# Rearranging the prologue of a sketched attention with feed-forward, and eight products on a tile of ones for TensorE

**The chip, the cores and the metric.** The kernel runs on one core of a Trainium2 chip. The metric is the device time of one execution in microseconds (us). A profile's span is about 1.8 us shorter than the time of the same execution (327.3 beside 329.06 us in the kernel before).

## The reference

The program is a sketched attention (batch 4, 4 heads, 1088 rows, 32 columns per head), whose output is the input of a gated feed-forward block on 4352 tokens.

```python
# S1, S2: 8 x 32 sketches; phi(x) = outer(S1 x, S2 x), 64 features
q_p, k_p = (phi(q), phi(k))
kv = np.einsum('bhsf,bhsd->bhfd', k_p, v)
z = np.sum(k_p, axis=2)
num = np.einsum('bhsf,bhfd->bhsd', q_p, kv)
den = np.einsum('bhsf,bhf->bhs', q_p, z)[..., None] + 1e-06
x = (num / den)                      # then to (4352, 128)
gate = 1.0 / (1.0 + np.exp(-(x @ w_gate)))
out = (gate * (x @ w_val)) @ w_out   # 128 -> 1536 -> 128
```

S1, S2 and the three weights come as 64-bit floats, which the kernel makes narrow with integer operations; the rest is 32-bit.

## The kernel before

The attention of one batch gives the tokens that the feed-forward block takes in chunks of 512. A chunk takes twelve waves: in a wave TensorE makes gate and value of one block of 128 hidden columns, ScalarE the sigmoid (`sg`), VectorE the product (`g`), and later TensorE adds it into `moeout`. The attention of later batches is done between waves. Before the first wave of all stands a prologue with nothing of the feed-forward block to fill it. Its order, the same for every engine, is that of the program:

```python
    # S is loaded (both on SyncE), made narrow, transposed, masked to sk ...
    turn_k(0, ((0, KBASE[2] + 1), (KBASE[2] + 1, T)))   # VectorE: kT, two parts
    turn_q(0, 0)                                        # VectorE: qT
    kps(0)                  # TensorE: kps = sk.T kT;  VectorE: kab = its transpose
    ab((0, 0, 0))           # TensorE: aps;  ScalarE: asb = copy of aps
    mult00 = ab((0, 1, 0), (0, 0, 0))
    mult10 = ab(None, (0, 1, 0), (psm, "wave"))
    for j0, j1 in ((0, 5), (5, NJK)):
        outer(0, 3, j0, j1)                             # GpSimd: kp of the last head
        for h in range(3):
            outer(0, h, j0, j1, nc.vector)              # VectorE: kp of three heads
        if j0 == 0:
            kv(0, [1, 2, 3, 4])                         # TensorE: kvz += v.T kp
    mult00()                                            # VectorE: qp = aps * bps
    mult10()
    kv(0, [5, 6, 7, 8, 0])                              # ... then ScalarE: kvd
    narrow_w(0, 0)
    narrow_w(1, 0)
    narrow_w(0, 1)
    ndt(0)                  # TensorE: ndps = kvd.T; VectorE: zb; ScalarE: nd
    narrow_w(2, 0)
    narrow_w(3, 0)
    invert = den(0, 0)      # TensorE: dps = zb.T qp
    divide = num(0, 0)      # TensorE: nps = nd.T qp
    invert()                # VectorE: dT, rc, rb
    divide()                # VectorE: xT = nps * rb
    narrow_w(0, 2)          # VectorE: w_sb of block 0
    narrow_w(1, 1)
    turn_q(0, 1)

    slot(None, 1)           # the first wave
    slot(lambda: r_group((0, 0, 1), None), 1)
    # ... cut ...
```

The narrowing of a tile is a chain over three engines, cut in steps by `yield`:

```python
        # step 0: cap (VectorE or GpSimd), tail (ScalarE)
        # step 1: two VectorE instructions make head, then:
        nc.scalar.activation(out=cap.bitcast(F32), in_=cap.bitcast(F32), func=ACTF.Square)
        nc.gpsimd.tensor_tensor(out=head, in0=head, in1=tail, op=ALU.add)
        yield
        # step 2: VectorE writes the narrow tile
```

The products of a wave and of `aps` and one of the `bps` share two buffers of PSUM (pool `psm`, tag `wave`), so one begins when the one before the last has been read.

Of the kernel before, what the change touches and what calls it, by code (L numbers as in the profile page):

```python
# [8 lines left out]
F32 = mybir.dt.float32  # L9
# [3 lines left out]
ALU = mybir.AluOpType  # L13
ACTF = mybir.ActivationFunctionType
MUL = ALU.mult

P = 128
# [3 lines left out]
def kernel(  # L21
# [12 lines left out]
    nc = tc.nc  # L34
# [11 lines left out]
    NJK = 9  # L46
# [34 lines left out]
    def narrow(out, bits, eng):  # L81




        n, m = out.shape[1:]
        lo, hi = bits[:, :, :, 0].bitcast(U32), bits[:, :, :, 1]

        def tmp(dt, tag, bufs):
            return sbN.tile([P, 3, P], dt, tag=tag, name=tag, bufs=bufs)[:, :n, :m]  # L90



        cap, tail = tmp(I32, "cap", 5), tmp(I32, "tail", 4)
        eng.tensor_scalar(
            out=cap.bitcast(F32), in0=hi.bitcast(F32), scalar1=122880.0, scalar2=-122880.0,
            op0=ALU.min, op1=ALU.max,
        )
        nc.scalar.activation(out=tail, in_=lo, func=ACTF.Copy, scale=2.0**-29)
        yield  # L100

        head = tmp(I32, "head", 3)
        nc.vector.tensor_scalar(  # L103
            out=head, in0=cap, scalar1=3, scalar2=0x3FFFFFF8,
            op0=ALU.logical_shift_left, op1=ALU.bitwise_and,
        )
        nc.vector.scalar_tensor_tensor(  # L107
            out=head, in0=cap, scalar=-0x40000000, in1=head, op0=ALU.bitwise_and, op1=ALU.bitwise_or
        )
        nc.scalar.activation(out=cap.bitcast(F32), in_=cap.bitcast(F32), func=ACTF.Square)  # L110
        nc.gpsimd.tensor_tensor(out=head, in0=head, in1=tail, op=ALU.add)  # L111
        yield

        nc.vector.scalar_tensor_tensor(  # L114
            out=out, in0=cap.bitcast(F32), scalar=1.265625 * 2.0**-30, in1=head.bitcast(F32),
            op0=ALU.is_ge, op1=MUL,
        )
        yield
# [3 lines left out]
    for n, s_ in enumerate((S1, S2)):  # L122
        rows = bass.AP(tensor=s_.tensor, offset=s_.offset, ap=[[0, P // R], [D, R], [1, D]])
        if wide:
            nc.sync.dma_start(
                out=sr_in[:, n].rearrange("p d w -> p (d w)"), in_=rows.bitcast(I32)
            )
        else:
            nc.sync.dma_start(out=sr[:, n], in_=rows)


    w_sb = const.tile([P, 3, NJ, P], F32, tag="w_sb", name="w_sb")
# [82 lines left out]
    ones = const.tile([P, 32], F32, tag="ones")  # L215
    nc.vector.memset(ones, 1.0)

    sig0 = const.tile([P, 1], F32, tag="sig0")
    nc.scalar.activation(out=sig0, in_=ones[:, :1], func=ACTF.Sigmoid)
    hm = const.tile([P, 2, R], F32, tag="hm")  # L220
    nc.vector.memset(hm, 0.0)
    for h in range(H):
# [4 lines left out]
    for n in range(2):  # L227
        t = const.tile([P, H, 32], F32, tag=f"zb{n}", name=f"zb{n}")
        nc.gpsimd.memset(t, 0.0)
        zb.append(t)  # L230

    if wide:
        for _ in narrow(sr, sr_in, nc.vector):
            pass

    sk = const.tile([P, 2, 2, R], F32, tag="sk")
    sab = []
    for n, inner in enumerate(([[1, R], [0, R]], [[0, R], [1, R]])):
        st_ = const.tile([P, 4, R], F32, tag=f"st{n}", name=f"st{n}")
        nc.vector.transpose(out=st_.rearrange("p u r -> p (u r)"), in_=sr[:, n])  # L240
        nc.vector.tensor_tensor(out=sk[:, :, n, :], in0=st_[:, :2, :], in1=hm, op=MUL)
        t = const.tile([P, R, R], F32, tag=f"s{n}", name=f"s{n}")
        nc.scalar.copy(
            out=t, in_=bass.AP(tensor=st_.tensor, offset=st_.offset, ap=[list(st_.ap[0])] + inner)
        )
        sab.append(t.rearrange("p i j -> p (i j)"))
    sa, sb = sab
    sk = sk.rearrange("p m n r -> p (m n r)")

    xT = const.tile([P, NTOK], F32, tag="xT")  # L250

# [37 lines left out]
    def w1():  # L289

        ci = moe["ci"]
        t0, tw = tok_chk[ci]
        jn = TCH // tw
        j0 = moe["w"] * jn
        wv = psm.tile([P, 2, TCH], F32, tag="wave", name="wave")
        if ci == 0:
            narrow_w(j0 + 4, 0)
            narrow_w(j0 + 2, 1)
            narrow_w(j0 + 1, 2)
        for which in range(2):  # L300
            for jj in range(jn):
                nc.tensor.matmul(  # L302
                    out=wv[:, which, jj * tw : (jj + 1) * tw],
                    lhsT=w_sb[:, which, j0 + jj, :],
                    rhs=xT[:, t0 : t0 + tw],
                    start=True,
                    stop=True,
                )
        sg = sbG.tile([P, TCH], F32, tag="sg", name="sg", bufs=3)
        nc.scalar.activation(out=sg, in_=wv[:, 0], func=ACTF.Sigmoid)  # L310


        def glu():
            g = sbG.tile([P, TCH], F32, tag="g", name="g")
            nc.vector.tensor_tensor(out=g, in0=wv[:, 1], in1=sg, op=MUL)  # L315
            moe["todo"].append((ci, j0, jn, g.rearrange("p (j t) -> p j t", j=jn)))

        moe["gate"] = glu
        moe["w"] += 1
        if j0 + jn == NJ:  # L320
            moe["ci"] += 1
            moe["w"] = 0
# [27 lines left out]

    kT_of, qT_of = {}, {}

    def turn_k(b, parts=((0, T),)):
        if b >= B:
            return
        kT = sbA.tile([P, T, 32], F32, tag="kT", name="kT")
        for t0, t1 in parts:
            nc.vector.transpose(  # L358
                out=kT[:, t0:t1].rearrange("p t s -> p (t s)"),
                in_=k_t[b][:, t0:t1].rearrange("p t d -> p (t d)"),  # L360
            )
        kT_of[b] = kT.rearrange("p t s -> p (t s)")

    def turn_q(b, n):
        if b >= B:
# [11 lines left out]
    def kps(b):  # L377
        t = ps2.tile([P, 2, 512], F32, tag="two", name="kps")
        for g in range(4):
            for pi in range(2):  # L380
                rows = slice(64 * pi, 64 * pi + 64)
                nc.tensor.matmul(  # L382
                    out=t[32 * g : 32 * g + 32, pi, : NJK * 32],
                    lhsT=sk[rows, :],
                    rhs=kT_of[b][rows, KBASE[g] * 32 : (KBASE[g] + NJK) * 32],
                    start=True,
                    stop=True,
                )

        KAB[b] = sbA.tile([P, 2, NJK, 32], F32, tag="kab", name="kab")  # L390
        for pi in range(2):
            nc.vector.transpose(  # L392
                out=KAB[b][:, pi].rearrange("p j c -> p (j c)"), in_=t[:, pi, : NJK * 32]
            )
        KP[b] = sbA.tile([P, H, NJK, F], F32, tag="kp", name="kp")

    def outer(b, h, j0=0, j1=NJK, eng=nc.gpsimd):
        a0 = KAB[b][:, h // 2, j0:j1, 2 * R * (h % 2) :]
        pst = list(a0.ap[0])
        jn = j1 - j0  # L400
        eng.tensor_tensor(  # L401
            out=KP[b][:, h, j0:j1].rearrange("p j (i l) -> p j i l", i=R),
            in0=bass.AP(tensor=a0.tensor, offset=a0.offset, ap=[pst, [32, jn], [1, R], [0, R]]),
            in1=bass.AP(tensor=a0.tensor, offset=a0.offset + R, ap=[pst, [32, jn], [0, R], [1, R]]),
            op=MUL,
        )

# [44 lines left out]
    def kv(b, j_list, zsum=None):  # L452
# [4 lines left out]
        for j in j_list:  # L457
            kr = 64 if j == 0 else P
            for which in range(2 if zsum is None else 1):
                for h in range(H):  # L460
                    nc.tensor.matmul(  # L461
                        out=kvz[32 * h : 32 * h + 32, F * which : F * which + F],
                        lhsT=v_t[b][:kr, h, j, :] if which == 0 else ones[:kr, :],
                        rhs=KP[b][:kr, h, j, :],
                        start=(j == 1 and which == 0),
                        stop=(j == 0),
                        skip_group_check=True,
# [22 lines left out]

    def sum_z(b):

        kp = KP[b]
        z4 = sbA.tile([P, H, 4, F], F32, tag="z4", name="z4", bufs=1)
        nc.gpsimd.tensor_tensor(out=z4, in0=kp[:, :, 1:5], in1=kp[:, :, 5:9], op=ALU.add)  # L495
        nc.gpsimd.tensor_tensor(out=z4[:, :, :2], in0=z4[:, :, :2], in1=z4[:, :, 2:], op=ALU.add)
        zs = sbA.tile([P, H, F], F32, tag="zs", name="zs")
        nc.gpsimd.tensor_tensor(out=zs, in0=z4[:, :, 0], in1=z4[:, :, 1], op=ALU.add)
        nc.gpsimd.tensor_tensor(out=zs[:64], in0=zs[:64], in1=kp[:64, :, 0], op=ALU.add)
        return zs  # L500

    def ndt(b):
# [79 lines left out]
        if m is not None:  # L582
            m()

    turn_k(0, ((0, KBASE[2] + 1), (KBASE[2] + 1, T)))
    turn_q(0, 0)
    kps(0)
    ab((0, 0, 0))
    mult00 = ab((0, 1, 0), (0, 0, 0))
    mult10 = ab(None, (0, 1, 0), (psm, "wave"))  # L590
    for j0, j1 in ((0, 5), (5, NJK)):
        outer(0, 3, j0, j1)
        for h in range(3):
            outer(0, h, j0, j1, nc.vector)
        if j0 == 0:
            kv(0, [1, 2, 3, 4])
    mult00()
    mult10()
    kv(0, [5, 6, 7, 8, 0])
    narrow_w(0, 0)  # L600
    narrow_w(1, 0)
    narrow_w(0, 1)
    ndt(0)
    narrow_w(2, 0)
    narrow_w(3, 0)
    invert = den(0, 0)
    divide = num(0, 0)
    invert()
    divide()
    narrow_w(0, 2)  # L610
    narrow_w(1, 1)
    turn_q(0, 1)

    slot(None, 1)
# [6 lines left out]
    slot(None, 1)  # L621
    slot(lambda: kps(1), 1)
    turn_q(1, 0)
    outer(1, 0)
    slot(lambda: r_group((1, 0, 0), None), 1)
    outer(1, 1)

    for b in range(1, B):
        more = b + 1 < B
# [2 lines left out]
        load_batch(b + 1)  # L632
        slot(lambda: r_group((b, 1, 0), (b, 0, 0)), wn)
        if b == 1:
            outer(b, 2)
        turn_q(b, 1)
        slot(lambda: r_group((b, 0, 1), (b, 1, 0)), wn)
        if b == 1:
            outer(b, 3)
        zs = sum_z(b)  # L640
        slot(lambda: r_group((b, 1, 1), (b, 0, 1)), wn)
        turn_k(b + 1)
        slot(lambda: kv(b, [1, 2, 3, 4, 5, 6, 7, 8, 0], zs), wn)
        if more:
            slot(lambda: kps(b + 1), wn)
            for h in range(H):
                outer(b + 1, h)
        turn_q(b + 1, 0)
        slot(lambda: ndt(b), wn)
        slot(lambda: r_group((b + 1, 0, 0) if more else None, (b, 1, 1)), wn)  # L650
# [41 lines left out]
```

## Time and profile before

| what | value |
|---|---|
| time, median of the first three runs | 330.79 us (330.24 to 330.87) |
| time and span of the profiled execution | 329.06 us, 327.3 us |
| TensorE busy | 307.6 us, 94% |
| first product; first, second, third wave begin | 7.36; 21.07, 26.23, 29.77 us |
| mean granted clock of TensorE | 0.986 |

A wait or a slow product in the prologue counts fully if the third wave begins later for it; after that TensorE has work without holes over 0.85 us. The prediction shows the lines.

### The profile page before, as it was taken

Reading aid. Unit: us, or ns where it says so; the run is one execution under the profiler, and the core shown is the slowest. Engines: PE = TensorE matmul, PEld = TensorE weight load, DVE = VectorE, ACT = ScalarE, POOL = GpSimd, SP = SyncE. Lnnn points to the kernel's source line nnn. Section 1 sums busy time; section 2 is a strip of 40 time slices with the busy share of each in tenths; the row PEclk is TensorE's granted clock in tenths of the full one; section 3 lists DMA queues with packets and bytes.
Section 4 is the critical chain, followed back from the end, with each engine's and each line's share of the span. In section 5 each row is a group of like instructions: output and inputs, shape, how many; then the busy total and the mean of one; then the engine's idle time right before and its main releaser. Section 6 shows DMA issues by size and latency. Waiting matters only on the chain.

```text
span 327.3 us, 3936 instructions
## 1 busy us (share of the span) xinstructions
PE 307.6 (94%) x1552; PEld 135.1 (41%) x1552; DVE 140.9 (43%) x252; ACT 86.4 (26%) x156; POOL 52.4 (16%) x59
## 2 busy tenths in 40 slices
PE   1869989999999999999999999999999999999993
PEld 0413333433344443434444434444444444444682
DVE  4875996645634432644313543242223233222321
ACT  3236344322222222122212221222222222222220
POOL 1345456856000190000000000000000000000000
PEclk9959999999999999999999999999999999999998
DMA  7999220240000200001000200010002000100010
GB/s 197 371 302 298 47 69 3 70 104 2 0 0 0 34 0 2 0 3 32 0 2 0 33 0 2 1 26 6 0 0 34 0 0 0 32 0 0 13 21 16
DMA packets 25586, 14.08 MB, mean 43 GB/s; under 512 B 19168, under 2 KB 22752, under 8 KB 25568
## 3 DMA queue, kind: packets, MB, share of 16 engines
q1 hardware_dynamic: 25424, 13.54, 15.7%
q10 hardware_dynamic: 144, 0.29, 0.3%
q8 instruction: 12, 0.20, 0.2%
q14 instruction: 6, 0.05, 0.1%
HBM read 11.60 MB, written 2.23 MB: 42 GB/s over the span
## 4 chain that ended last, share of the span: by engine, by line
PE 87%; DVE 6%; DMA 3%; SPq 1%; ACT 1%; issue 1%; DVEq 0%; ACTq 0%
PE wave L302 52%; PE moeout L260 27%; PE aps L424 2%; DMA w_in<-in_moe_w_out_dram 2%; PE dps L525 2%; DMA w_in<-in_moe_w_val_dram 1%; PE kvz L461 1%; PE nps L560 1%; DVE g L315 1%; DVE w_sb L114 1%; DVE head L107 1%; PE bps L424 1%; SPq L188 1%; DVE rb L543 0%; DVE head L103 0%
## 5 line engine op out<-in xcount | busy, mean ns | idle before, releaser
L302 PE MATMUL wave<-xT,w_sb 128*128 128x512 f32 (+1 forms) x432 | 193.2, 574 | 3.5 <-DVE w_sb L114 2.0
L315 DVE TENSOR_TENSOR g<-wave,sg 128x512 f32<-128x512 f32 x102 | 69.9, 685 | 124.1 <-ACT sg L310 123.8
L302 PEld LDWEIGHTS wave<-xT,w_sb 128*128 128x128 f32 x432 | 81.6, 191 | 98.5 <-issue 84.4
L310 ACT ACTIVATE sg<-wave 128x512 f32<-128x512 f32 x102 | 60.8, 596 | 198.6 <-PE wave L302 198.6
L260 PE MATMUL moeout<-g,w_sb 128*128 128x512 f32 (+1 forms) x216 | 106.2, 584 | 0.5 <-DVE g L315 0.5
L260 PEld LDWEIGHTS moeout<-g,w_sb 128*128 128x128 f32 x216 | 38.2, 189 | 44.1 <-issue 37.8
L401 POOL TENSOR_TENSOR kp<-kab 128x576 f32<-128x576 f32 (+2 forms) x14 | 15.5, 1133 | 43.6 <-DVE kab L392 43.6
L443 DVE TENSOR_TENSOR qp<-bps,asb 128x512 f32<-128x512 f32 (+1 forms) x16 | 11.5, 722 | 23.3 <-PE bps L424 17.7
L111 POOL TENSOR_TENSOR head<-head,tail 128x384 int32<-128x384 int32 (+1 forms) x13 | 13.8, 1064 | 25.9 <-DVE head L107 15.7
L424 PE MATMUL aps<-qT,s 32*64 32x256 f32 (+1 forms) x128 | 12.1, 443 | 1.6 <-DVE qT L370 1.6
L434 ACT COPY asb<-aps 128x512 f32<-128x512 f32 (+1 forms) x16 | 9.8, 612 | 7.0 <-PE aps L424 5.4
L110 ACT ACTIVATE cap<-cap 128x384 f32<-128x384 f32 (+1 forms) x13 | 6.5, 502 | 18.7 <-DVE head L107 18.7
L424 PE MATMUL bps<-qT,s 32*64 32x256 f32 (+1 forms) x128 | 11.4, 425 | 0.0
L382 PE MATMUL kps<-kT,sk 64*32 64x288 f32 x64 | 3.9, 482 | 7.4 <-DVE kT L358 7.4
L570 DVE TENSOR_TENSOR xT<-nps,rb 128x512 f32<-128x512 f32 (+1 forms) x8 | 5.8, 724 | 10.6 <-PE nps L560 10.4
L424 PEld LDWEIGHTS aps<-qT,s 32*64 32x64 f32 x128 | 3.8, 138 | 14.0 <-issue 5.5
L461 PE MATMUL kvz<-kp,v 128*32 128x64 f32 (+1 forms) x288 | 7.0, 222 | 0.7 <-DVE kp L401 0.6
L495 POOL TENSOR_TENSOR z<-kp 128x1024 f32<-128x1024 f32 x3 | 7.4, 2476 | 0.2
L107 DVE SCALAR_TENSOR_TENSOR head<-cap,head 128x384 int32<-128x384 int32 (+1 forms) x13 | 7.1, 549 | 0.4
L461 PEld LDWEIGHTS kvz<-kp,v 128*32 128x32 f32 (+1 forms) x288 | 5.5, 109 | 4.2 <-DVE kp L401 1.5
L270 DVE STREAM_TRANSPOSE o_sb<-moeout 128x512 f32<-128x512 f32 (+1 forms) x9 | 6.1, 678 | 2.5 <-PE moeout L260 2.5
L536 DVE STREAM_TRANSPOSE dT<-dps 128x256 f32<-128x256 f32 (+1 forms) x8 | 3.7, 463 | 7.5 <-PE dps L525 7.5
(47 smaller groups left out, 98.0 us busy)
## 6 DMA issues: line engine op xcount, KB each, us to landing
v<-in_v_dram SPq DMA_DIRECT2D x16, 144.0 KB, 5.7
k<-in_k_dram SPq DMA_DIRECT2D x3, 544.0 KB, 6.2
q<-in_q_dram SPq DMA_DIRECT2D x3, 544.0 KB, 7.9
w_in<-in_moe_w_gate_dram SPq DMA_DIRECT2D x6, 256.0 KB, 5.4
w_in<-in_moe_w_val_dram SPq DMA_DIRECT2D x6, 256.0 KB, 5.5
w_in<-in_moe_w_out_dram SPq DMA_DIRECT2D x6, 256.0 KB, 5.6
out_dram<-o_sb SPq DMA_DIRECT2D x20, 64.0 KB, 2.0
k<-in_k_dram ACTq DMA_DIRECT2D x1, 288.0 KB, 2.7
```

What stands on the lines that cost most here:

```text
L107: nc.vector.scalar_tensor_tensor(out=head, in0=cap, scalar=-0x40000000, in1=head, op0=ALU.bitwise_and, op1=ALU.bitwise_or)
L111: nc.gpsimd.tensor_tensor(out=head, in0=head, in1=tail, op=ALU.add)
L260: nc.tensor.matmul(out=moe["acc"][:, :tw], lhsT=w_sb[:, 2, j, :], rhs=g[:, jj, :tw], start=(j == 0), stop=(j == NJ - 1),)
L302: nc.tensor.matmul(out=wv[:, which, jj * tw : (jj + 1) * tw], lhsT=w_sb[:, which, j0 + jj, :], rhs=xT[:, t0 : t0 + tw], start=True, stop=True,
L310: nc.scalar.activation(out=sg, in_=wv[:, 0], func=ACTF.Sigmoid)
L315: nc.vector.tensor_tensor(out=g, in0=wv[:, 1], in1=sg, op=MUL)
L401: eng.tensor_tensor(out=KP[b][:, h, j0:j1].rearrange("p j (i l) -> p j i l", i=R), in0=bass.AP(tensor=a0.tensor, offset=a0.offset, ap=[pst ...
L424: nc.tensor.matmul(out=dst[64 * c : 64 * c + 64, m, : 32 * tn], lhsT=sx[rows, :], rhs=qT_of[bb][rows, t0 : t0 + tn, c, :], start=True, sto ...
L434: nc.scalar.copy(out=ASB[a_of][:, :, :w], in_=aps[:, :, :w])
L443: nc.vector.tensor_tensor(out=QP[bb][:, 2 * pr : 2 * pr + 2, 32 * t0 : 32 * t0 + w], in0=bps[:, :, :w], in1=ASB[b_of][:, :, :w], op=MUL,)
L461: nc.tensor.matmul(out=kvz[32 * h : 32 * h + 32, F * which : F * which + F], lhsT=v_t[b][:kr, h, j, :] if which == 0 else ones[:kr, :], rh ...
L495: nc.gpsimd.tensor_tensor(out=z4, in0=kp[:, :, 1:5], in1=kp[:, :, 5:9], op=ALU.add)
```

## The change

Its intent is twofold: to shorten the prologue by another order of its work, and to keep TensorE's clock up by products of a tile of ones, whose result nobody reads, wherever TensorE would idle. The diff, cut to its core:

```diff
@@ narrow: one more step, between VectorE's part and that of ScalarE and GpSimd
+        yield
         nc.scalar.activation(out=cap.bitcast(F32), in_=cap.bitcast(F32), func=ACTF.Square)
@@ the loads of S1 and S2: one on SyncE, one on ScalarE
-            nc.sync.dma_start(
+            (nc.sync, nc.scalar)[n].dma_start(
@@ products of ones
+    def warm(*cols):
+        t = psm.tile([P, 2, 512], F32, tag="wave", name="warm")
+        ... for n in cols: ...
+            nc.tensor.matmul(out=t[:, 0, :n], lhsT=x, rhs=r, start=True, stop=True)
+    warm(512, 512, 512)            # behind the memset of ones
@@ narrowing of S, transposes (cut): one transpose and one sk for both S, and
+    turn_k(0, 0, KBASE[2] + 1)     # first half of kT in the hole of the narrowing
+    next(steps, None)
+    ...
+    turn_k(0, KBASE[2] + 1, T)     # second half behind sk
     mult10 = ab(None, (0, 1, 0), (psm, "wave"))
+    warm(256)
     for j0, j1 in ((0, 5), (5, NJK)):
-        outer(0, 3, j0, j1)
-        for h in range(3):
-            outer(0, h, j0, j1, nc.vector)
+        for pi in range(2):                       # two heads in one instruction
+            outer(0, pi, 0, 2, j0, j1, nc.vector)
         if j0 == 0:
             kv(0, [1, 2, 3, 4])
+    narrow_w(0, 0)
+    kv(0, [5, 6, 7, 8, 0])
     mult00()
     mult10()
-    kv(0, [5, 6, 7, 8, 0])
-    narrow_w(0, 0)
+    narrow_w(0, 1)
+    warm(256)
+    ndt(0)
+    warm(256)
+    narrow_w(0, 2)
     narrow_w(1, 0)
-    narrow_w(0, 1)
-    ndt(0)
+    invert = den(0, 0)
+    divide = num(0, 0)
+    warm(512, 512)
     narrow_w(2, 0)
     narrow_w(3, 0)
-    invert = den(0, 0)
-    divide = num(0, 0)
     invert()
+    narrow_w(0, 3)
     divide()
-    narrow_w(0, 2)
     narrow_w(1, 1)
+    narrow_w(1, 2)
     turn_q(0, 1)
@@ later batches: GpSimd's outer products in pairs of heads, the same sums (cut)
```

## The prediction

> **What bounds the kernel now.** I read the page's slices first. TensorE is busy 94% of the span, and from the fourth slice on it is full and at full clock; what it lacks is at the beginning.
>
> ```profile
> PE   1869989999999999999999999999999999999993
> PEclk9959999999999999999999999999999999999998
> ```
>
> A slice is 8.2 us. The first row is TensorE's busy share in tenths, the second the clock granted to it. Three slices are short of work and the third (16.4 to 24.5 us) ran at about half clock. So I took the chain of waits in order of time (start, us, what), to see what leads to the point from which TensorE never rests.
>
> ```profile
> 17.35 0.68 PE dps L525 x8
> 18.06 0.46 DVE dT L536
> ...
> 19.04 0.72 DVE rb L543
> ...
> 20.46 0.56 DVE w_sb L114
> 21.02 0.04 issue
> 21.07 3.75 PE wave L302 x4
> 24.82 0.69 PE aps L424 x8
> ...
> 25.53 0.65 ACT asb L434
> 26.18 0.04 issue
> 26.23 1.98 PE wave L302 x4
> ```
>
> The first wave (four products of 512 columns for the feed-forward block) begins at 21.07 and takes 3.75 us; the second takes 1.98, and later ones 1.72. From 26.23 on, TensorE's timeline has no gap over 0.1 us until 47.9 and four in all, of 0.85, 0.79, 0.73 and 0.55. The 327.29 - 26.23 = 301.1 us after the second wave's start are therefore fixed by TensorE's work, which the change leaves as it is. **The question is how much earlier the second wave starts.** Before it stands a serial prologue; VectorE's timeline shows it:
>
> ```profile
> 4.41 0.20 DVE L95 TENSOR_SCALAR cap<-sr_in 128x64 f32<-128x64 f32 x1 [3.06 <-DMA sr_in<-in_S_dram]
> ...
> 5.60 0.23 DVE L114 SCALAR_TENSOR_TENSOR sr<-cap,head 128x64 f32<-128x64 f32 x1 [0.51 <-POOL head L111]
> ...
> 6.53 1.36 DVE L358 STREAM_TRANSPOSE kT<-k 128x576 f32<-128x576 f32 x2
> 7.82 0.67 DVE L370 STREAM_TRANSPOSE qT<-q 128x512 f32<-128x512 f32 x1
> 9.20 0.85 DVE L392 STREAM_TRANSPOSE kab<-kps 128x288 f32<-128x288 f32 x2 [0.71 <-PE kps L382]
> 9.97 3.93 DVE L401 TENSOR_TENSOR kp<-kab 128x320 f32<-128x320 f32 x6
> 13.83 1.27 DVE L443 TENSOR_TENSOR qp<-bps,asb 128x512 f32<-128x512 f32 x2
> ```
>
> In brackets is the idle time before a group and what ended it. VectorE waits for the sketches S until 4.41, makes them narrow with a hole of 0.51 us, and then transposes k, waits for TensorE's kps, and spends 3.9 us on the outer products kp. The clock comes from the windows view (stretch; PE, PEld, DVE, ACT, POOL busy with counts; clock; DMA share; GB/s):
>
> ```profile
> 17.00:18.00 1.00, 0.65 (x16) 0.22 (x22) 0.00 (x0) 1.00 (x4) 1.00 (x3) 0.92 1.09 398
> 18.00:19.00 1.00, 1.00 (x17) 0.16 (x16) 0.88 (x3) 0.21 (x1) 0.39 (x1) 0.50 1.04 412
> 24.00:25.00 1.00, 1.00 (x5) 0.21 (x8) 0.52 (x2) 0.66 (x2) 0.78 (x1) 0.67 0.98 323
> ```
>
> 0.92 and 0.67 put the fall to half at 17.84 and the return at 24.67. Nothing is recorded before 11.01, but the products tell: kps take 0.68 us each at 7.36 and 0.43 (the median of all kps) later, so the start was at half clock too.
>
> [...]it is released 3.65 us after the first product, the slow spell lasts 6.83 us[...], and follows 3.4 us in which TensorE was busy 56% (gaps of 0.49 and 1.01 us). [...]kp on VectorE takes 0.41 us at the least (256 elements, GpSimd idle), but 0.91 and 1.02 for 320 beside GpSimd's part of the same work. [...]The two S loads are issued one after the other at 0.73 and 1.48 and land 2.9 us later.
>
> **The change, part by part.**
> Loads of S: the second moves to ScalarE's queue, so it is issued 0.75 earlier; S should be there near 3.7, VectorE starts at 3.75 instead of 4.41. The first part of k is issued behind it, 0.7 later; it landed 2.7 after issue (3.4) and will land near 4.3 to 4.7[...].
> Narrowing S: cap and two head instructions end 0.69 after their start (4.41 to 5.10), so 4.45. The first half of kT fills the hole while GpSimd adds: 0.69 (half of 1.36, rounded), to about 5.2, or 5.5 if k is late. Then sr 0.25, one transpose instead of two 0.25, one sk instead of two 0.2, the second half of kT 0.65. The second half of kps starts at about 6.7 instead of 7.95: **1.25 gained**.
> Three products on ones at the start: one of 512 columns is 0.43 us at full clock (1.72 / 4 in a later wave) and 0.86 at half. They run from 1.0 to 3.6[...]. I expect the release then[...], and that it still holds at kps, though TensorE idles from 3.6 to 6.2. Kps at full clock saves about 0.5 of 1.2 us: kab starts at 7.45 instead of 9.20, **1.75 gained**.
> Outer products: six on VectorE and two on GpSimd become four on VectorE, two of 640 and two of 512 elements[...]. GpSimd's first cap of the weights falls near 10.5 to 11 (the first weights' last part landed at 10.9) and may cost up to 0.35, as in kp of 256 elements at 0.76 beside a cap. I take 0.15. They end at 11.1 instead of 13.9: **2.75 gained**, a further 1.0.
> kv's second part keeps its 1.57 us from the last kp to kvd (13.90 to 15.47), all of it at full clock already: kvd at 12.7.
> ScalarE's order: before, nd waited until 17.04 behind two tails and a square, though ndps was done at 16.34. Now they come after it: **0.65 more, 3.4 in all**, dps at about 13.95. The two single products about ndt must fit: each is 0.21 at full clock for 256 columns, beside the 0.42 for kvd and 0.5 for zb or nd. The first also waits for VectorE's qp (12.4), which is done when kv ends. I take no cost.
> From dps to the first wave VectorE does the same work in another order (w_sb before xT): 3.72 us, first wave at 17.7 instead of 21.07. The two products of 512 beside it (0.86 at full clock) end before that.
> First wave at full clock: 1.72 instead of 3.75. **Most of these 2.0 us are not on the path.** The second wave needs the buffer of the first, so sg and g, and before sg ScalarE squares the next weights (24.14 to 24.66, after VectorE's heads). Sg started at 24.86 because of the wave, and could have at 24.58. So 0.28 comes through. Sum at the second wave: 3.4 + 0.28 = 3.7, start at 22.5.
> The other parts (GpSimd's outer products in pairs, the sum over kp in the new layout, the same steps of narrowing cut in four) lie in stages where GpSimd is idle over half the time: 0.
>
> **The rivals.**
> (a) The clock falls again between the first and the second wave. By the above TensorE is done with aps at about 20.1 and waits until 22.5 on VectorE and ScalarE, a hole of 2.4 us which no product fills, and before the first wave is a smaller one. [...]Against it: [...]whoever chose five products will have watched the clock. If it falls, the second wave and what follows run 3.4 us or so at half clock, 1.7 lost: gain 2.0, 328.8 us. I give it one chance in three: 0.6 us. The same may happen at the start, so that kps run at half clock after all: 0.5 lost, one in three, 0.15.
> (b) The inserted products hold up the real ones: at half clock they last twice as long, and two of them wait for a buffer that VectorE or ScalarE has to read first. Worth up to 1 us, gain 2.7, 328.1. The chosen places and sizes speak against it.
> (c) The prologue is bound by transfers: DMA share is 1.0 from 4 us on, so moved issues bring nothing, and late k or weights eat a part. S, k and q are the first in the queue, and the weights of the first product (10.9) are not needed before 11; worth up to 0.7.
> (d) All the hidden time comes through, as when the 2.0 us of the first wave count fully: gain 5.4, 325.4. It needs VectorE's stretch between dT and w_sb of the second column (18.06 to 24.52, without a gap) to be shorter, and nothing removed lies in it.
>
> **The range and the chances.** 330.8 - 3.7 + 0.6 + 0.15 = 327.85, so 327.8. The low end, 326.0, is (d) nearly; the high end, 329.5, is (a) with most of (b). Two per cent faster is 324.2, so 6.6 us: the second wave would start at 19.6, before VectorE could have the inputs; 3 in 100. Slower by 2% needs a loss of more than 6.6 in a prologue that the change shortens: 1 in 100.
>
> **What would show it.** Kab on VectorE near 7.45, four kp in about 2.8 us, nd right after ndps, dps near 14, first wave near 17.7 in about 1.75 us, second near 22.5 with TensorE idle before it, and from there the old distance of 301 us to the end. A clock of 0.5 after 18 us would show (a), one about 7 us its smaller brother. The prediction is wrong if the second wave starts early by much more or less than 3.7, or if the 301 us change.

The marked cuts, here and in the expectations below, took out rules that no trace or run of this case shows. The sum: 3.7 us at the second wave, made of 1.25 before kps, 0.5 by kps at full clock, 1.0 by the outer products, 0.65 by nd and 0.28 by the first wave; less 0.6 and 0.15 for rival (a), a gain of 3.0 and a time of 327.8 us. A spell of 3.4 us at half clock, as in rival (a), was measured later, from 24.75 to 28.16 us in experiment 15.

## The result, and the profile after

The changed kernel takes 326.17 us (325.97 to 326.53, 4 runs), the kernel before 330.83 us (330.24 to 331.99, 4 runs). Ratios in this document are the mean time of one kernel's runs over that of the other's of the same rounds, so not quite the ratio of the medians: 0.9851 here, with a 95% interval of 0.9827 to 0.9875, which is within 2%. The forecast was a gain of 3.0 us, 327.8 us. The measured 4.7 us put the median at the lower edge of the range, and the ratio (0.9851 x 330.79 = 325.9 us) puts the time below it.

The slices of the changed kernel's page, busy TensorE and its clock in tenths per 8.1 us:

```profile
PE   7879989999999999999999999999999999999993
PEclk9999999999999999999999999999999999999998
```

The third slice, which had a clock of 0.5, has 9, and TensorE works from the first slice on. Its timeline (start, us, engine, line, operation, count; in brackets the idle time before) shows the products on ones and the first two waves:

```profile
0.95 5.13 PE L226 MATMUL warm<-ones 128*128 128x512 f32 x6 [0.95 <-DVE hm L232]
6.75 1.31 PE L375 MATMUL kps<-kT,sk 64*32 64x288 f32 x16 [0.67 <-DVE sk L591]
...
10.51 0.70 PE L226 MATMUL warm<-ones 128*128 128x256 f32 x2 [0.28 <-ACT asb L429]
...
18.14 1.99 PE L226 MATMUL warm<-ones 128*128 128x512 f32 x4
19.97 1.88 PE L296 MATMUL wave<-xT,w_sb 128*128 128x512 f32 x4
...
23.70 1.98 PE L296 MATMUL wave<-xT,w_sb 128*128 128x512 f32 x4 [1.21 <-ACT asb L429]
```

The count says something that the prediction missed: three products are six instructions. So what the program writes as one product of 512 columns, in 32 bits, costs here two instructions of 0.43 us at full clock (1.72 us for the four of a later wave), 0.86 together, and 1.71 at half (two of 0.85 to 0.86; the starts are at 1.96, 2.82 and 3.67 us), twice what was reckoned. The first three run until 6.08, to within 0.7 us of kps, and the last two (1.99 us) hold up the first wave, whose xT is there at 18.97, until 19.97. The second wave begins at 23.70 instead of 26.23. VectorE's timeline up to zb:

```profile
3.17 0.19 DVE L95 TENSOR_SCALAR cap<-sr_in 128x64 f32<-128x64 f32 x1 [1.82 <-DMA sr_in<-in_S_dram]
...
5.31 0.78 DVE L352 STREAM_TRANSPOSE kT<-k 128x576 f32<-128x576 f32 x1 [1.46 <-DMA k<-in_k_dram]
...
8.13 0.85 DVE L385 STREAM_TRANSPOSE kab<-kps 128x288 f32<-128x288 f32 x2 [0.19 <-PE kps L375]
8.90 2.72 DVE L396 TENSOR_TENSOR kp<-kab 128x640 f32<-128x640 f32 x4
11.54 1.28 DVE L438 TENSOR_TENSOR qp<-bps,asb 128x512 f32<-128x512 f32 x2
...
14.52 0.34 DVE L512 COPY zb<-ndps 64x4 f32<-64x4 f32 x2 [0.84 <-PE ndps L501]
```

S is there at 3.17, but now VectorE waits 1.46 us for the first part of k. The four outer products take 2.72 us, where about 2.8 were forecast. From kv to nd, and again before the second wave, the path runs over ScalarE:

```profile
13.56 0.37 ACT L479 COPY kvd<-kvz 128x256 f32<-128x256 f32 x1 [1.14 <-PE kvz L456]
14.95 0.27 ACT L514 COPY nd<-ndps 128x128 f32<-128x128 f32 x1 [1.02 <-DVE zb L512]
...
22.11 0.52 ACT L111 ACTIVATE cap<-cap 128x384 f32<-128x384 f32 x1 [1.21 <-DVE head L107]
```

Nd waits for VectorE's zb (14.52 to 14.86), not for ndps alone, which ends at 14.48. Dps follows nd because it takes the same buffer of PSUM as ndps (pool `ps1` has one). Then the chain of waits (start, us, what) gives the rest of the way:

```profile
15.36 0.64 PE dps L521 x8
...
16.56 1.01 issue
17.57 0.69 PE nps L556 x10
18.28 0.69 DVE xT L566
...
22.63 0.49 ACT sg L304
23.12 0.54 ACT asb L429
23.65 0.04 issue
23.70 1.98 PE wave L296 x4
```

Nps has a hole of 1.01 us for which the profile shows no wait. It costs about 0.1, because VectorE's w_sb ends at 18.20 anyway. Nor does the first wave's late start hold up the second: sg comes behind ScalarE's square (22.11 to 22.63), which waited for VectorE's head, and the first wave had ended at 21.85. Set beside each other (start in us; the end for kp):

| event | before | predicted | after |
|---|---|---|---|
| cap of S on VectorE | 4.41 | 3.75 | 3.17 |
| kab | 9.20 | 7.45 | 8.13 |
| last kp ends | 13.90 | 11.1 | 11.62 |
| kvd | 15.47 | 12.7 | 13.56 |
| dps | 17.35 | 13.95 | 15.36 |
| first wave | 21.07 | 17.7 | 19.97 |
| second wave | 26.23 | 22.5 | 23.70 |
| end of the span | 327.3 | | 324.8 |

From the second wave to the end it is 301.1 us in both. So **between the two profiles the gain is only 2.5 us**, less than the 3.7 of the prediction's sum, and yet the timed gain is 4.7. Both differences had to be explained: why the prologue shrank by less, and where the other 2.1 us are.

### The profile page after: what moved, and what is told of

It is laid out like the page before. It is cut to its first block, busy times and chain, and to the rows that moved or that the text cites. A ratio compares the mean times of both kernels' runs of the same rounds, so it can differ in the third digit from the quotient of the medians.

```text
span 324.8 us, 3960 instructions
## 1 busy us (share of the span) xinstructions
PE 312.4 (96%) x1568; PEld 137.7 (42%) x1568; DVE 139.2 (43%) x248; ACT 86.4 (27%) x156; POOL 49.8 (15%) x53
## 4 chain that ended last, share of the span: by engine, by line
PE 87%; DVE 8%; DMA 1%; issue 1%; ACT 1%; POOL 0%; ACTq 0%; DVEq 0%; POOLq 0%
PE wave L296 51%; PE moeout L253 27%; PE aps L419 2%; PE nps L556 2%; PE dps L521 2%; DVE head L107 1%; DMA k<-in_k_dram 1%; PE kvz L456 1%; PE bps L419 1%; DVE g L309 1%; PE kps L375 1%; DVE head L103 1%; DVE w_sb L115 1%; DVE qT L363 1%; DVE qp L438 1%
## 5 line engine op out<-in xcount | busy, mean ns | idle before, releaser
L396 POOL TENSOR_TENSOR kp<-kab 128x576 f32<-128x576 f32 (+1 forms) x8 | 13.2, 1670 | 39.3 <-DVE kab L385 39.3
L419 PE MATMUL aps<-qT,s 32*64 32x256 f32 (+1 forms) x128 | 11.3, 413 | 1.7 <-DVE qT L363 1.6
L111 ACT ACTIVATE cap<-cap 128x384 f32<-128x384 f32 (+1 forms) x13 | 6.5, 503 | 17.7 <-DVE head L107 17.7
L226 PE MATMUL warm<-ones 128*128 128x512 f32 (+1 forms) x16 | 9.1, 696 | 1.2 <-DVE hm L232 1.0
L95 POOL TENSOR_SCALAR cap<-w_in 128x384 f32<-128x384 f32 x12 | 6.5, 550 | 7.6 <-DMA w_in<-in_moe_w_out_dram 7.6
L556 PE MATMUL nps<-qp,nd 64*32 64x256 f32 (+1 forms) x128 | 6.1, 401 | 1.0 <-issue 1.0
```

Of the source, the lines that this page charges most:

```text
L226: nc.tensor.matmul(out=t[:, 0, :n], lhsT=x, rhs=r, start=True, stop=True)
L396: eng.tensor_tensor(out=o0.rearrange("p j m (i l) -> p (j m) i l", i=R), in0=bass.AP(tensor=a0.tensor, offset=a0.offset, ap=[pst] + jm + [ ...
L419: nc.tensor.matmul(out=dst[64 * c : 64 * c + 64, m, : 32 * tn], lhsT=sx[rows, :], rhs=qT_of[bb][rows, t0 : t0 + tn, c, :], start=True, sto ...
L556: nc.tensor.matmul(out=nps[32 * h : 32 * h + 32, c, :w], lhsT=ND[b][rows, 32 * h : 32 * h + 32], rhs=QP[b][rows, h, 32 * t0 : 32 * t0 + w] ...
```

## The experiments

Sixteen experiments ran, some of them one kernel profiled again; all gave the right result. They came in four lots, each on one chip with the kernel before beside it; its medians there were 330.28, 329.82, 330.05 and 329.60 us, 11 runs each. Theory A: the clock makes most of the gain, and the kernel before loses more by it in its usual runs than in the profiled one. The first rival, R1: the rearrangement carries the gain and the products only fill idle time.

**1. The changed kernel without its products.**

```diff
-    warm(512, 512, 512)
...  and the calls of warm(256) x3 and warm(512, 512) likewise
```

> The changed kernel without its eight products on ones: the rearrangement alone. Theory A (the clock makes the larger part, and the kernel before loses 3.4 us of slow clock more in its usual runs than in the profiled one): the slow spells are back, TensorE is released only after kps begin, the first wave is slow again, and the time is 329.0 us (328.0 to 330.2), with a granted mean clock of 0.98 to 0.99. Rival R1 (the rearrangement carries the gain, the products only fill idle time): 326.5 us, within 0.7 of the changed kernel.

Measured: 328.86 us (328.31 to 329.06), ratio 0.9961 (0.9939 to 0.9984), mean clock 0.987. In the profile kps take 1.81 us again, the first release is at 14.90 us only, kv ends at 15.24, and the first wave takes 3.78. So the rearrangement alone is worth 1.3 us (0.39% of 330; 0.5 to 2.0 by the interval); R1 falls.

**2. The kernel before with the products, nothing rearranged.**

```diff
+    warm(512, 512, 512)
...  warm(256) behind mult10, before and behind ndt(0); warm(512, 512) behind num(0, 0)
```

> The kernel before with the eight products at the corresponding places and nothing rearranged. Theory A: full clock from about 5.6 us on, kps in 1.3 instead of 1.8 us, no slow spell; about 1.7 us from the slow spell of the usual runs and 0.6 from the start: 328.3 us (327.6 to 329.0). R1: 330.8, within 0.5 of the kernel before. Both parts add up to the whole gain of 4.7 us within 0.5 if they don't work on the same wait.

Measured: 329.28 us (328.92 to 330.43), ratio 0.9987 (0.9960 to 1.0015): a miss, and a gain that is not clear of zero. The products end at 5.60, but in the old order kps begin at 7.86:

```profile
7.86 1.78 PE L391 MATMUL kps<-kT,sk 64*32 64x288 f32 x16 [2.26 <-DVE kT L367]
```

The clock is released at 4.62, falls at 8.03 and comes back at 11.45, so kps run at half clock as before. The second wave begins at 26.23, where it does without the products in the first profile; that the two agree so closely is chance, since S was there 0.5 us later in this one (4.91). Alone the two parts give 1.3 and 0.4 us, together 3.8 (experiment 8, on another chip), and on this chip the rearrangement with only three of the products 3.1 (experiment 3): **each needs the other**. The rearrangement brings kps closer behind the first products, 0.67 us instead of 2.26, and there the clock held.

**3 and 4. The changed kernel with the first three, or with the last five products only.**

```diff
 a3:  -    the calls of warm(256) x3 and warm(512, 512)
 a4:  -    warm(512, 512, 512)
```

> The changed kernel with the first three products only. If release at the start is what counts and TensorE's own work then holds the clock: 326.3 us, slow spell absent. If the five later ones are needed to hold it: the clock falls after a window with the gaps between kv and the first wave, near 18 to 22 us, and the second wave runs slow: 327.8 us (327.2 to 328.5). My estimate is the second.

> The changed kernel with the five later products only. Theory A: kps and the first aps run at half clock (kps begin 6.7, take 1.8 instead of 1.3 us), released at about 10 to 11, held from there: 326.9 us (326.5 to 327.5). R1: no change, 326.2. Rival R2 (the early release is what matters, the five are idle): as without any products, 329.

Measured: the first three alone 327.06 us (326.04 to 327.36), ratio 0.9907 (0.9883 to 0.9931); the last five alone 329.00 us (328.04 to 331.12), ratio 0.9981 (0.9949 to 1.0013). The three bring it to 3.1 us, between my two expectations and just under the range of the second. The five without the three are worth nothing over the bare rearrangement, as rival R2 had it and against Theory A. In the profile the release comes at 13.04 only, and until then the product before kv runs at half clock in kv's way (kv begins at 12.44, ends at 15.05). But this profile is of the fastest of the six runs (328.04 us); why the others are 0.7 to 3.1 us slower is not shown. Mean clocks of 0.998 beside 329 us warn of a trap in reading: the clock's records begin with the first release, so the half clock before it counts as full in the mean (in the kernel before, released at 11.01, the windows view says 1.00 from 8 to 9 us, where kps take 0.68 us instead of 0.43).

**5 to 7. The kernel before, profiled three more times; 8. the changed kernel on that chip.** No edits.

> The kernel before, profiled again (first of three). Theory A, to explain that the timed gain (4.7 us) is larger than the gain between the two profiled spans (2.5 us): the kernel before takes 329.0 to 331.7 us[...], and its first profile caught the fast end. A profile with a time above 330 us must then show more slow clock (10 us or more after the first release instead of 6.8) or a slower start (kab on VectorE or kv's end later), with the second wave later by as much as the time is longer. Rival: the times differ with the same clock records and the same second wave; then transfers or the launch are the cause.

> As the first look: time minus 329.06 equals the delay of the end of the second or third wave against the first profile within 0.3 us, if theory A holds, and the clock records differ. If all three looks fall at 329.0 to 329.6 with the same records, theory A stays unshown by profiles.

> As the first two looks: a time above 330 us goes with a later second or third wave and with other clock records than in the first profile, if theory A holds.

> The changed kernel on the same chip with five rounds: 326.2 us with a spread of under 0.8 us, while the kernel before spreads over 2 us.[...]

| profile of | time | first release | half clock again | kv ends | second wave begins, takes | third wave |
|---|---|---|---|---|---|---|
| before, first | 329.06 | 11.01 | 17.84 to 24.67 | 15.40 | 26.23, 1.98 | 29.77 |
| before, look 1 | 330.67 | 16.43 | 19.84 to 26.67 | 16.69 | 27.82, 1.98 | 31.37 |
| before, look 2 | 331.74 | 13.76 | 20.58 to 30.82 | 15.69 | 27.06, 3.78 | 32.40 |
| before, look 3 | 329.97 | 15.49 | 18.91 to 25.73 | 16.21 | 27.11, 1.98 | 30.66 |
| changed, first | 326.53 | 5.60 | never | 13.49 | 23.70, 1.98 | 27.24 |
| changed, again | 326.01 | 3.93 | never | 13.13 | 23.15, 1.98 | 26.70 |

The time less the start of the third wave is 299.3 us in every row, to 0.04. The changes of the clock in a row lie 3.41 us apart or a multiple of it, to 0.02: 3.41 from 16.43 to 19.84, 6.83 from 11.01 to 17.84, 10.24 from 20.58 to 30.82 (falls behind the last product, as at 325.05 us in the first row, are left out). So the kernel before has no single time: it spreads over 2.7 us by where its spells of half clock fall (and a little by when S lands, 4.41 to 4.75 on VectorE), and the profile I predicted from was at its fast end. In look 2 the chain of waits shows two slow waves instead of one:

```profile
21.35 3.78 PE wave L302 x4
27.06 3.78 PE wave L302 x4
32.56 1.72 PE wave L302 x4
```

And the windows view (stretch, its length, busy us and counts of PE, PEld, DVE, ACT, POOL, then clock, DMA share, GB/s) shows the same stretch in look 2, then in the changed kernel:

```profile
24.00:28.00 4.00, 3.24 (x11) 0.81 (x10) 2.78 (x6) 2.66 (x5) 2.11 (x3) 0.50 0.99 314
```

```profile
24.00:28.00 4.00, 4.00 (x24) 1.40 (x23) 2.58 (x6) 2.31 (x5) 1.65 (x2) 1.00 1.02 337
```

The changed kernel took 326.37 us (326.01 to 326.63), ratio 0.9886 (0.9859 to 0.9914). Its mean clock was at least 0.995 in all six runs, and its spread 0.6 us, as expected. The kernel before beside it spread from 329.02 to 331.87, with clocks of 0.981 in its two slowest runs (331.44 and 331.87). The gain is then about 3.8 us. The kernel before has a mean of 329.9 to 330.1 us (11 runs each), in the first result 331.0 (4 runs): the other 0.9 of the 4.7 us is luck of which runs those four were, or of their chip.

**9. K before S on ScalarE's queue.**

```diff
-    for n, s_ in enumerate((S1, S2)):  # both loads of S first
+    load_s(0)
+    ...                                # k's first part on ScalarE's queue
+    load_s(1)
```

> The changed kernel with ScalarE's queue issuing the first part of k before the second S. In the changed kernel VectorE idled 1.46 us for that part, which landed at 5.3 us[...]. Theory K (the late k cost the prediction some 0.7 us): k lands near 3.5, S near 3.3, kT begins right after the head instructions, and kps can begin as soon as the three products end at 6.1; kab at 7.4 instead of 8.1, 325.6 us (325.2 to 325.9). Rival: S lands as much later as k earlier, and nothing is gained: 326.2.

Measured: 327.18 us (326.33 to 329.77), ratio 0.9931 (0.9895 to 0.9967): slower than the changed kernel, though not clear of noise (the two intervals just overlap; the slowest run is 3 us off). The rival was right, and worse than reckoned: k landed at 3.7, and the S behind it at 5.7 only. VectorE's and TensorE's timelines of the profiled run (328.61 us, the second slowest of six):

```profile
5.80 0.20 DVE L95 TENSOR_SCALAR cap<-sr_in 128x64 f32<-128x64 f32 x1 [4.45 <-DMA sr_in<-in_S_dram]
```

```profile
0.95 4.78 PE L230 MATMUL warm<-ones 128*128 128x512 f32 x6 [0.95 <-DVE hm L236]
7.83 1.80 PE L379 MATMUL kps<-kT,sk 64*32 64x288 f32 x16 [2.11 <-DVE sk L595]
```

TensorE idles 2.11 us between the products and kps. The clock fell at 8.29 and came back at 11.71, and kps took 1.80 us.

**10. Without the single product before kv.**

```diff
     mult10 = ab(None, (0, 1, 0), (psm, "wave"))
-    warm(256)
```

> The changed kernel without the single product of 256 columns after the second qp's matmuls. Theory W (it holds up kv: it waits for ScalarE's copy until 10.51 and ends at 11.2, while kv could begin at 10.4): kvd 0.4 to 0.5 us earlier, the second wave too, 325.7 us (325.4 to 326.0), and the clock still holds. Rival: the clock falls without it in some runs, median 326.5 with a wider spread[...].

Measured: 326.02 us (325.81 to 328.15), ratio 0.9891 (0.9861 to 0.9921). Kvd begins at 13.25, 1.57 us after the last kp, the distance of the kernel before; with the product it is 1.94. So theory W holds in its mechanism, with a time just above its range: the product, which waits for ScalarE's copy until 10.51, costs the path 0.4 us. But one of six runs took 328.15 with a clock of 0.991. I read that as the price: the product also carries the clock over a hole (that run has no profile, so this is not shown). On balance nothing is gained.

**11. Both, with a shorter start.**

```diff
-    warm(512, 512, 512)
+    warm(512, 512, 256)
...  and the edits of 9 and 10
```

> Both: k first, no product before kv, and the first three products shortened to 512, 512, 256 columns so that they end at 5.2 us instead of 6.1. If the three waits are one after the other the gains add: k 0.8, the shorter start 0.4, kv 0.5, so 324.6 us (324.2 to 325.2), the best of all. If the clock isn't released by the shorter start, kps run at half clock and the median is 325.3 with a spread of over 1 us.

Measured: 328.72 us (325.96 to 330.15), ratio 0.9952 (0.9907 to 0.9996): a clear miss. In the profiled run (330.15 us) TensorE idled from 5.40 to 6.94, the clock fell at 8.49 for 6.8 us and again at 25.56. The best of its runs, 325.96, is no better than the changed kernel's.

**12. The outer products of the last head back on GpSimd.**

```diff
-        for pi in range(2):
-            outer(0, pi, 0, 2, j0, j1, nc.vector)
+        outer(0, 1, 1, 2, j0, j1)
+        outer(0, 0, 0, 2, j0, j1, nc.vector)
+        outer(0, 1, 0, 1, j0, j1, nc.vector)
```

> The changed kernel with the outer products of the last head given back to GpSimd (VectorE one of two heads and one of one head, GpSimd one, in each half), as before. [...]kp on VectorE again takes near 3.8 us instead of 2.7 though VectorE has a quarter less to do, kvd comes 1.0 us later, and the time is 327.2 us (326.8 to 327.6). If the contention came from the caps of the weights alone, kp takes 2.1 us and the time falls to 325.8.

Measured: 326.36 us (325.82 to 326.45), ratio 0.9888 (0.9861 to 0.9915): the same as the changed kernel, and a miss. The kp group on VectorE, and GpSimd's beside it:

```profile
8.97 3.10 DVE L396 TENSOR_TENSOR kp<-kab 128x640 f32<-128x640 f32 x4
```

```profile
9.13 2.06 POOL L396 TENSOR_TENSOR kp<-kab 128x320 f32<-128x320 f32 x2 [4.79 <-DVE kab L385]
```

VectorE is slower beside GpSimd's part: it takes 3.10 us for three quarters of the work instead of 2.72 for all of it, and kp ends 0.45 later (12.07). But kvd begins at 13.64 instead of 13.56. Kv's 72 products stream on TensorE without a hole from 11.14 to 13.49 in the changed kernel, behind the product that holds them up; the 0.45 us are hidden behind them. Moving the outer products is worth nothing as the kernel stands.

**13 to 15. The first three products only, profiled three more times.** No edit to experiment 3. Open was why the clock does not fall about the first wave, for which I had counted a loss.

> The changed kernel with the first three products only, profiled again. Theory H (the five later products hold the clock): in a run near 327 us the record shows half clock for 3.4 or 6.8 us, beginning between 17 and 24 us, after a window with the holes about ndt and the first wave, and the second or third wave is later by the lost time. Rival: full clock throughout at 327 us, and the difference lies in when S and k land.

> As the other looks at this kernel: a time near 327 us goes with a spell of half clock after 17 us if theory H holds, a time near 326.0 us with none.

> As the other looks at this kernel: a time near 327 us goes with a spell of half clock after 17 us if theory H holds, a time near 326.0 us with none.

Measured: 326.71, 327.37 and 327.83 us, each with a spell of half clock: 15.75 to 22.57, 16.75 to 23.58, and 24.75 to 28.16. The profile of experiment 3 (326.04 us) had none. The third waves begin 0.66, 1.33 and 1.78 us later than in that profile, and the times are 0.67, 1.33 and 1.79 longer. Two windows of look 3:

```profile
16.00:20.00 4.00, 2.36 (x12) 0.80 (x6) 3.54 (x9) 0.80 (x3) 0.48 (x2) 0.59 1.06 398
20.00:24.00 4.00, 3.76 (x12) 0.86 (x10) 2.96 (x6) 2.02 (x5) 3.07 (x4) 0.55 1.07 235
```

Theory H holds: **without the five later products the clock falls in most executions**, at one of two places: the holes about ndt (looks 2 and 3), or the one before the second wave, 21.38 to 23.41 in look 4. In experiment 3 the five slower runs had mean clocks of 0.986 to 0.993 beside 0.996 in the fast one. With them it held in every one of the ten runs of the changed kernel, by mean clocks of 0.995 or more. They cost 0.5 us when all goes well (326.04 against 326.53 in the two profiles with full clock and the same landing of k), 0.34 of it at kvd by the product before kv, and save up to 1.8. Which of the other four are needed was not tested.

**16. Both S on SyncE, k's first part first on ScalarE.**

```diff
-            (nc.sync, nc.scalar)[n].dma_start(
+            nc.sync.dma_start(
```

> The changed kernel with both S loads on SyncE's queue, as before, and k's first part first on ScalarE's. S lands at 4.3 instead of 3.1, k at 3.4 instead of 5.3. Theory K: the two changes nearly cancel, VectorE's head instructions end at 5.1, kT's first half at 5.8, sk at 6.5: kps begin at 6.55 instead of 6.75 and the time is 326.1 us (325.7 to 326.5), so that the split of S is worth nothing by itself. If S matters more than k, 326.9 or more, with the clock at risk as in the k-first run because kps begin over 1 us after the three products.

Measured: 326.55 us (326.28 to 326.79), ratio 0.9897 (0.9876 to 0.9918), 0.2 us off the changed kernel on another chip, and just above what was expected. S was used at 4.60 and k landed at 3.5; kps began at 6.64 instead of 6.75. Splitting S over two queues moves the wait from S to k and is worth nothing by itself.

## Why the prediction was right or wrong

**Right.** What counts is the start of the second wave, with a fixed rest: 301.1 us in both profiles, and 299.3 after the third wave in all that I compared. The time of the outer products (about 2.8 forecast, 2.72 measured), though of the 1.0 us booked for them little reaches kvd by experiment 12; the release of the clock by the first products before kps (5.60 against 6.75 us); the first wave's slowness as mostly hidden (its 2 us fell away, and the way from dps to the second wave became 0.5 us shorter, for 0.28 reckoned); and 2% as out of reach.

**The step that failed most is the last sum, "330.8 - 3.7 + 0.6 + 0.15".** It took shifts read off one profile from the median of other runs. The profiled execution had taken 329.06 us, which the record showed. The 1.7 us between it and the median are mostly clock, as far as the looks show (the runs of the median have no profile): they have the kernel before at 329.06 to 331.74 us, with other clock records each time and S up to 0.3 later. The change removes this spread as well. In numbers: the shift between the profiles is 2.53 us (329.06 - 326.53), and the two profiled runs lie 1.77 below and 0.36 above their medians; 2.53 + 1.77 + 0.36 = 4.66, the whole gain. Part of the 1.77 is luck: in the other lots the mean of the kernel before lies 0.8 to 1.0 above 329.06. The prediction treated the clock as a risk of the changed kernel alone (rival a), never as a variable loss of the kernel before.

**Rival (a), with a third of a chance and 0.6 us, did not happen,** and its partner at the start (0.15) neither. The hole reckoned at 2.4 us before the second wave is 1.21. The likely reason is a wrong size: "one of 512 columns is 0.43 us" is one of two instructions, so the last two products take 1.99 us instead of 0.86 and push the first wave into the hole, which is 2.04 us without them in the profile of experiment 3. The first three, reckoned to end at 3.6, end at 6.08, where they meet kps. Without the later five the rival does happen, as the looks 13 to 15 show. The wrong size made the change look weaker at its purpose than it is. Nor can the places where the clock changes be counted on: the first release came at 11.01, 16.43, 13.76 and 15.49 us in the four profiles of one kernel.

**The sum of 3.7 us was too large by 1.2,** in three places. Kab was 0.7 late: "the first part of k ... will land near 4.3 to 4.7" was 5.3 (its load took 3.9 us instead of 2.7 beside S and the other part of k), and VectorE stood still for it; experiments 9 and 16 show that neither order of the two loads does better. "Kv's second part keeps its 1.57 us" was 1.94, because the product before kv blocks it, by experiment 10; rival (b) was right to this extent. "Nd right after ndps", 0.65 us, was not to be had: nd begins 0.09 us after zb ends, in all the profiles in which nothing else held up ScalarE, as the wait on VectorE shows. The profile before had it: zb ended at 16.71 there, so that nd, at 17.04, could begin only some 0.2 us sooner, and 0.2 is what was gained (from the end of ndps to nd 0.70 us before, 0.47 after). With all three, dps was 1.4 late. Against these stand 0.2 us more than reckoned between dps and the second wave.

**Rival (c) was half right:** the moved load brought no time, because k's first part landed at 5.3 us instead of 3.4. Rival (d) was wrong in its reason though its time, 325.4, is near the measured one.

The prediction's account of the change as parts that add up has fallen too: alone the two bring 1.3 and 0.4 us, together 3.8 on the chip where the changed kernel was run again. What the new order of ScalarE's work and k's first transpose in the hole of the narrowing bring each was not tested.

What a single hole must look like for the clock to fall stays open in part. I cut the eighteen traces into windows of 3.41 us, the step at which their own clock records change, and left out the fall behind the last product. Of some 1,600 windows at full clock, twelve were followed by half clock, all with TensorE busy 34 to 57%. Three others, busy 45 to 54%, were not, and none busy 58% or more was. In the kernel before a window of 3.41 us with TensorE busy 56% (14.43 to 17.84 us, gaps of 0.49 and 1.01) was followed by a fall; in the profile of experiment 3 the window from 21.34 to 24.75, busy 45% in large products, was not, and in look 4 the same stretch, busy 40%, was. Below 58%, busy time in the profile thus does not decide alone.

## What to carry to other kernels

Before you subtract anything, compare the profiled run with the median, and take several profiles where the prologue has holes: part of the time may be a lottery over where the clock falls (329.06 to 331.74 us here), and a change can win by ending it. Products that hold the clock work only if real work follows soon (here a hole of 0.67 us behind the first three was harmless, as were 1.26 us without work between 4 and 8 us in experiment 15, and with holes of 1.54 us and more, in experiments 11, 9 and 2, the clock fell in the profiles), so they and the order of the work have to be tuned together, and judged by the spread of many runs. A wait shortened ahead of a stream that is bound elsewhere, as the outer products ahead of kv, gains nothing.
